# A sparse-attention, mixture-of-experts and feed-forward kernel: local attention of three batches regrouped into units of 18 blocks of 32 queries

## The chip, the cores and the metric

The kernel runs on one core of a Trainium2 chip. The metric is device time in microseconds (us) of one execution, median of several runs.

## The reference

Three stages follow one another on 4 x 576 = 2304 tokens of 512 features, all in f32.

```python
# attention: 4 batches, 8 heads, 576 positions, head size 64
rel = pos[:, None] - pos[None, :]
mask_local = (rel >= 0) & (rel < 32)
mask_strided = (rel >= 0) & (pos[None, :] % 32 == pos[:, None] % 32)
masks = [mask_local for heads 0..3] + [mask_strided for heads 4..7]
attn = softmax(where(masks, q @ k.T / 8, -1e9)); out = attn @ v
# mixture: 8 experts, 1024 wide, weights of the tokens from 8 Sinkhorn rounds over all tokens
out += P[:, e:e+1] * (relu(x @ w1[e]) @ w2[e])
# feed-forward, 2048 wide
h = x @ w_in; return (h * sigmoid(1.702 * h)) @ w_out
```

## The kernel before

The tokens are cut into three blocks of 768. A block passes through the 32 units of the mixture (eight experts, four units of 256 hidden columns each), and later through the units of the feed-forward stage. A unit is a Strassen-like scheme of seven products on two-part (high and low) f32r operands, each product six matmuls of 128x384 (line 1067), and six down products a unit (lines 1333 to 1335). In the code a product or a down product is a *piece*; a unit has 13 places for pieces. `pieces` lists them in order, `advance` runs the next one and the side tasks hung on it (splits of weights, sums of weights on GpSimd, sums of inputs).

The attention of block 0 (batch 0 and the first 192 positions of batch 1) must be there before the first pieces can run on it, and its second half (positions 384 to 767) before the twelfth piece: the first 26 pieces run two units on the first half of the block, then on the second. The rest of the attention is woven between pieces. Heads are taken in pairs; pairs 0 and 1 are local, pairs 2 and 3 strided. A strided ("compact") pair is one group: 64 score products of 32x18 (line 673), mask and maximum on VectorE, one exponential on ScalarE, the sum on VectorE, scaling on GpSimd (line 717), a transpose on VectorE (line 726), copies into `wide`, 16 value products (line 752). A local pair is three groups, each of two tiles of 96 queries against 128 keys, both heads: four score products (line 783), mask and maximum (lines 798, 808), four exponentials with accumulated sums (line 815), scaling on GpSimd (line 830), four transposes on TensorE (line 838), a copy (line 845 or 847), four value products (line 857), a copy into `x` (line 869).

The order is written by hand at the start: `START` is a list of tokens, where S, M, L, E, D, N, T, C, V, K with a group's number are scores, mask, maximum, exponential, sum, scaling, transposes, copy, values and keep; i and a number are that many idle products (line 1480); q and v are loads; W and Y split weights, X the input; P is `advance`. After its 16 pieces `att_step` takes one group a step through a pipeline that is four steps deep, and calls `fill` three times a step, which advances 1.5 pieces on average. After the last step the gate's products and the Sinkhorn rounds follow, between pieces.

TensorE's accumulation banks are few: `pa` serves transposes and one of the two value halves of a compact group, `y` (two buffers) the other half, local values and the down products. Every engine runs its instructions in the written order.

## Time and profile before

| | |
|---|---|
| median of 3 runs | 1942.31 us (1939.58 to 1944.88) |
| the profiled execution | 1940.98 us, span 1939.2 us |
| TensorE (PE) busy | 1907.1 us, 98% |
| VectorE (DVE) | 1454.4 us, 75% |
| GpSimd (POOL) | 1244.9 us, 64% |
| ScalarE (ACT) | 851.8 us, 44% |
| share of the chain that ended last | PE 65%, DVE 2%, POOL 1%, DMA 1% |
| mean granted TensorE clock | 0.997 |

The span is the time from the first to the last instruction of the profiled execution; the shares say how much of it each engine was busy. An engine that is busy all the time bounds the whole, but a share is a mean over stages, so the stages are read apart: rows by windows give each engine's busy time in a stretch, the granted TensorE clock (1.00 is 2.4 GHz, 0.50 is 1.2 GHz) and what the DMA engines moved. An "idle before" with a releaser is a wait, and names who ended it.

### The profile page before, as it was taken

The numbers are of one execution on the slowest core, as the hardware profiler recorded it, in microseconds if no ns is written. First come the engines' busy times: TensorE is split into PE (matmuls) and PEld (weight loads), VectorE is DVE, ScalarE is ACT, GpSimd is POOL, SyncE is SP. The second block draws the span as 40 slices with busy tenths as digits, with TensorE's granted clock in tenths as the row PEclk, the third lists the DMA queues.
The fourth block names the chain that finished last, engine by engine and source line by source line (L and its number), as shares of the span: only waits on it lengthen the run. The fifth ranks groups of instructions, "written<-read, shape, count | busy, mean of one in ns | idle before, by whom it ended". The sixth has DMA issues, their size and how long they took to land.

```text
span 1939.2 us, 35075 instructions
## 1 busy us (share of the span) xinstructions
PE 1907.1 (98%) x11687; PEld 1783.2 (92%) x11687; DVE 1454.4 (75%) x2715; ACT 851.8 (44%) x2079; POOL 1244.9 (64%) x1282
## 2 busy tenths in 40 slices
PE   8999999999999999999999999999999999999999
PEld 6787888888888999999999999999999998888988
DVE  7787687777767788788877788888886766656555
ACT  5555456677664433333333333333333445534332
POOL 4465666777776767677768878888888767601100
PEclk9999999999999999999999999999999999999999
DMA  8477789999997989888888789999989867655653
GB/s 285 146 265 268 257 290 341 353 352 352 353 322 252 333 285 307 291 297 290 288 269 293 255 313 315 319 332 339 347 306 334 284 219 269 239 187 191 223 188 120
DMA packets 284451, 546.18 MB, mean 282 GB/s; under 512 B 30864, under 2 KB 52720, under 8 KB 283376
## 3 DMA queue, kind: packets, MB, share of 16 engines
q1 hardware_dynamic: 280816, 532.08, 79.6%
q10 hardware_dynamic: 3456, 11.87, 1.9%
q8 instruction: 94, 1.54, 0.3%
q14 instruction: 85, 0.70, 0.1%
HBM read 382.30 MB, written 161.53 MB: 280 GB/s over the span
## 4 chain that ended last, share of the span: by engine, by line
PE 65%; DVE 2%; POOL 1%; DMA 1%; issue 0%; ACT 0%; SPq 0%; ACTq 0%; DVEq 0%
PE y L1228 22%; PE pA L1067 18%; PE pC L1067 9%; PE pB L1067 5%; PE y L1335 4%; PE y L1334 4%; PE y L1333 4%; DMA w<-s7moe 1%; DMA w<-s1moe 0%; POOL s L1200 0%; POOL comb L1175 0%; DVE comb L1175 0%; POOL xc L589 0%; DVE xc L593 0%; DVE r L1181 0%
## 5 line engine op out<-in xcount | busy, mean ns | idle before, releaser
L1067 PE MATMUL pA<-xc,w 128*128 128x384 f32 x2880 | 571.9, 335 | 2.7 <-DVE pB L1123 2.1
L1228 PE MATMUL y<-comb,w 128*128 128x384 f32 x2688 | 537.6, 334 | 1.7 <-DVE sum L1238 1.0
L1067 PEld LDWEIGHTS pA<-xc,w 128*128 128x128 f32 x2880 | 507.5, 188 | 20.0 <-DVE pB L1123 3.5
L1228 PEld LDWEIGHTS y<-comb,w 128*128 128x128 f32 x2688 | 472.0, 188 | 3.2 <-DVE sum L1238 2.5
L1175 POOL TENSOR_TENSOR comb<-s,comb 128x384 fp32r<-128x384 f32 x256 | 282.8, 1115 | 88.0 <-ACT comb L1170 79.8
L1238 DVE TENSOR_TENSOR sum<-y,sum 128x384 f32<-128x384 f32 x420 | 230.9, 550 | 96.7 <-PE y L1228 94.6
L1067 PE MATMUL pC<-xc,w 128*128 128x384 f32 x1464 | 295.0, 336 | 0.5 <-issue 0.5
L1335 PE MATMUL y<-w,hl 128*128 128x512 f32 x672 | 268.5, 400 | 4.9 <-DVE hl L1107 4.6
L1067 PEld LDWEIGHTS pC<-xc,w 128*128 128x128 f32 x1464 | 258.9, 188 | 10.5 <-issue 0.9
L1333 PE MATMUL y<-w,hh 128*128 128x512 f32 x672 | 265.0, 394 | 1.6 <-DVE x L869 0.7
L1334 PE MATMUL y<-w,hh 128*128 128x512 f32 x672 | 266.3, 396 | 0.0
L1170 ACT ACTIVATE comb<-r 128x384 fp32r<-128x384 f32 x192 | 101.0, 526 | 364.2 <-DVE r L1181 348.0
L1335 PEld LDWEIGHTS y<-w,hl 128*128 128x128 f32 x672 | 126.5, 188 | 36.2 <-DVE hl L1107 9.0
L1333 PEld LDWEIGHTS y<-w,hh 128*128 128x128 f32 x672 | 126.8, 189 | 21.5 <-DVE acc L1348 1.4
L1067 PE MATMUL pB<-xc,w 128*128 128x384 f32 x708 | 143.2, 337 | 0.0
L1334 PEld LDWEIGHTS y<-w,hh 128*128 128x128 f32 x672 | 126.6, 188 | 15.9
L1175 POOL TENSOR_TENSOR comb<-r,comb 128x384 fp32r<-128x384 f32 x64 | 67.5, 1054 | 114.2 <-ACT comb L1170 114.2
L278 ACT ACTIVATE w<-raw 128x256 fp32r<-128x256 f32 (+1 forms) x307 | 135.7, 460 | 7.2 <-POOL raw L242 6.9
L272 POOL TENSOR_TENSOR w<-raw,w 128x512 fp32r<-128x512 f32 (+1 forms) x104 | 122.3, 1192 | 24.2 <-ACT w L278 23.7
L1170 ACT ACTIVATE comb<-s 128x384 fp32r<-128x384 f32 x256 | 131.6, 514 | 11.0 <-POOL s L1200 11.0
L1200 POOL TENSOR_TENSOR s<-r,r 128x384 f32<-128x384 f32 x127 | 134.3, 1077 | 2.5 <-DVE r L1181 2.0
L1362 DVE TENSOR_TENSOR acc<-y,acc 128x512 f32<-128x512 f32 x126 | 86.7, 688 | 63.1 <-PE y L1335 63.0
(178 smaller groups left out, 2800.4 us busy)
## 6 DMA issues: line engine op xcount, KB each, us to landing
w<-s1moe SPq DMA_DIRECT2D x448, 256.0 KB, 4.9
w<-s7moe SPq DMA_DIRECT2D x448, 256.0 KB, 4.9
s1moe<-w SPq DMA_DIRECT2D x216, 256.0 KB, 5.0
w<-s1ffn SPq DMA_DIRECT2D x133, 256.0 KB, 2.8
s7moe<-kw SPq DMA_DIRECT2D x116, 256.0 KB, 4.7
s7moe<-w SPq DMA_DIRECT2D x96, 256.0 KB, 4.8
w<-s2ffn SPq DMA_DIRECT2D x38, 512.0 KB, 3.8
raw<-wa SPq DMA_DIRECT2D x32, 512.0 KB, 6.0
```

The source lines that it names most:

```text
L272: eng.tensor_tensor(out=t[:, 1], in0=src, in1=f(high), op=ALU.subtract)
L278: nc.scalar.activation(out=high, in_=src, func=AF.Copy)
L1067: nc.tensor.matmul(out=o, lhsT=w[:, hw, kk * P : (kk + 1) * P], rhs=x[:, hx, kk, :], start=opens and m == 0, stop=ends and m == len(todo) - 1,
L1170: nc.scalar.activation(out=t[:, 0, :], in_=part[i, q], func=AF.Copy)
L1175: eng.tensor_tensor(out=t[:, 1, :], in0=part[i, q], in1=f(t[:, 0, :]), op=ALU.subtract)
L1200: eng.tensor_tensor(out=part[i, q], in0=part[i, a], in1=part[i, b], op=op)
L1228: nc.tensor.matmul(out=o, lhsT=t[:, hw, dt * P : (dt + 1) * P], rhs=x[:, hx, :], start=(n == 0), stop=(n == 5))
L1238: nc.vector.tensor_tensor(out=a, in0=o, in1=a, op=ALU.add)
L1333: nc.tensor.matmul(out=o, lhsT=hh[:, c], rhs=w[:, 0], start=(m == 0), stop=False)
L1334: nc.tensor.matmul(out=o, lhsT=hh[:, c], rhs=w[:, 1], start=False, stop=False)
L1335: nc.tensor.matmul(out=o, lhsT=hl[:, c], rhs=w[:, 0], start=False, stop=(m == 1))
L1362: nc.vector.tensor_tensor(out=a, in0=y, in1=a, op=ALU.add)
```

## The change

Batch 0 keeps its local pairs in 96-query tiles (functions now called `tile_...`). In batches 1 to 3 a local pair is one unit: 18 blocks of 32 queries, each against the 64 keys of its own and the previous block, both heads. Scores are 40 products of 32x64 on eight sub-array positions (20 block places, the last two repeated), in the layout [128, 5 x 128]; mask (two instructions) and maximum on VectorE, the subtraction of the maximum on GpSimd, one exponential over 640 columns on ScalarE, the sum on VectorE, the scaling on GpSimd; transposes in two parts (12 blocks in three, 6 blocks in two), written back into `e` by ScalarE; values in 36 products of 64x32 on two sub-array positions. Value tiles of these pairs are laid out anew (18 blocks of 64 keys, 576 KB instead of 384 KB). The compact pairs are as before, with one buffer for their transposed tile instead of two.

The groups become 20 instead of 32, in the order local, compact, local, compact. A step now has four fills of 2.8 pieces and finishes a group one step after its scores. `START` is written anew and goes through 13 groups; it still has 16 pieces, and 34 idle products instead of 24. The tiles' masks are loaded apart, and all masks and constants on SP's queue.

```diff
 START = (
-    "S0 M0 i2 S1 L0 M1 E0 L1 i2 S2 E1 D0 N0 M2 q12 L2 i3 T0:p D1 S4 E2 N1 C0 M4 V0:B L4 T1:p D2 S3 E4 M3 "
...
-    "E9 M10 X3 i2 S12 W211 A2 C7 D9 i1 P1 B1 L10 N9 V7:pB M12 E10 T9 P2 K7 C9 P3 D10 L12 N10 S11 P4 E12 "
-    "M11 L11 P5 Y11 Y10 V9:pB E11 K9 P6 D11 T10:p D12 N11 X6 P7 N12 C10 T11:p S13 V10:B q22 C11 P8 K10 "
-    "M13 V11:B K11 P9 XX21 T12:p S14 P10 L13 C12 P11 E13 M14 P12 S15 q20 D13 i1 P13 L14 N13 M15 E14 L15 "
-    "P14 i3 P15 "
+    "S0 M0 i2 S1 L0 M1 E0 i2 S2 L1 E1 D0 M2 N0 L2 q10 i3 T0:p D1 E2 N1 C0 D2 i2 V0:p S5 K0 N2 T1:p M5 q12 "
...
+    "M9 X3 V6:p E7 S8 D7 v10 q11 L9 q13 K6 P N7 P E9 T7:B M8 "
+    "D9 P P N9 C7 L8 P V7:p Y10 Y11 T9 v11 K7 P S10 C9 M10 P U8 q20 V9:pB E8 S11 L10 D8 P U10 q22 K9 M11 "
+    "P N8 E10 T8:p C8 L11 P V8:p E11 K8 G8:B R8 D11 i1 H8:p D10 N11 S12 v20 T11 q21 N10 M12 C11 J8 i3 "
+    "T10:B L12 G10:p R10 V11:yy U12 C10 V10:p K11 E12 K10 X6 H10:B XX21 v22 J10 i6 P P P P P "
 ).split()
-RATE = 1.5
+RATE = 2.8
...
-        eT = ap.tile([P, 4, P], F32, tag="eT", name="eT")
+        eT = ap.tile([P, 4, P], F32, tag="eT", name="eT", bufs=1)
...
+    def att_scores(i, b, pair):
+        qkt = att_in["qk", b, pair]
+        sc = eps.tile([P, 2, 512], F32, tag="sc", name="sc")
+        for m in range(LM):
+            for c in range(CG):
+                w = min(m * CG + c, NBLK - 1)
+                k0 = max(0, w - 1) * Q
+                for j in range(2):
+                    nc.tensor.matmul(
+                        out=sc[c * Q : (c + 1) * Q, j, m * WIN : (m + 1) * WIN],
+                        lhsT=qkt[j * HD : (j + 1) * HD, 0, w * Q : (w + 1) * Q],
+                        rhs=qkt[j * HD : (j + 1) * HD, 1, k0 : k0 + WIN],
+                        start=True,
+                        stop=True,
+                        tile_position=(j * HD, c * Q),
+                    )
...
+        def below():
+            nc.gpsimd.tensor_tensor(
+                out=s, in0=s, in1=st[:, 0, :, None].to_broadcast([P, 2 * LM, WIN]), op=ALU.add
+            )
...
+    def att_values(i, b, pair, part, banks="y"):
+        av = named_bank(banks[0], "av")
+        lo, hi = (0, PART) if part == 0 else (PART, NBLK)
+        for w in range(lo, hi):
+            for j in range(2):
+                rows = slice(j * HD, (j + 1) * HD)
+                nc.tensor.matmul(
+                    out=av[rows, (w - lo) * Q : (w - lo + 1) * Q],
+                    lhsT=vt[rows, w, :],
+                    rhs=e[rows, w * Q : (w + 1) * Q],
+                    start=True,
+                    stop=True,
+                    tile_position=(j * HD, j * HD),
+                )
...
+    MIXED = (0, 2, 1, 3)
+    groups = [(0, 0, 0), (0, 1, 0), (0, 2), (0, 0, 1), (0, 1, 1), (0, 3), (0, 0, 2), (0, 1, 2)]
+    groups += [(b, pair) for b in range(1, B) for pair in MIXED]
+    NLIST = len(groups) - 4 * (B - 2) + 1
+    NSTEP = len(groups) + 1
...
-        for t in run(2, att_normalise):
-            t()
-        first, apart = run(4, att_values), 4 <= i < n + 4 and groups[i - 4][2] < 0
-        if apart:
-            for t in first:
                 t()
-            first = ()
-            fill()
-        second, third = run(3, att_transpose), run(0, att_scores)
-        for t in first + second:
-            t()
-        if not apart:
-            fill()
-        for t in third[:1]:
-            t()
-        run(1, att_exp)
-        loads_of(i)
+        go(run(1, "normalise"))
+        fill()
+        go(run(1, "transpose", 0))
+        scores = run(0, "scores")
+        go(scores[:1])
+        fill()
+        go(run(1, "transpose", 1))
+        go(run(1, "values", 0))
+        go(scores[1:])
+        fill()
+        go(run(1, "values", 1))
+        run(0, "exp")
         fill()
-        for t in third[1:]:
-            t()
-        fill()
+        loads_of(i)
...
-        nc.scalar.dma_start(out=msk, in_=masks)
+        nc.sync.dma_start(out=spare[1], in_=masks0)
         load_qk(*EARLY[1], begin)
-        nc.scalar.dma_start(out=cst, in_=consts)
...
+        load_qk(0, MIXED[1])
+        nc.sync.dma_start(out=msk, in_=masks)
+        nc.sync.dma_start(out=cst, in_=consts)
```

How the order on the engines moves is seen at three places. First TensorE before the twelfth piece. `pt` are transposes, `av` values, `sc` scores, `idle_out` idle products, `pA` and `pC` products, `y` down products. Before:

```order
L838 MATMUL pt<-cst,e 128x96 x4
L783 MATMUL sc<-qkt 96x128 x4
L1067 MATMUL pC<-xc,w_630 128x384 x6
L1067 MATMUL pA<-xc,w_390 128x384 x6
L1333 MATMUL y<-w_902,hh_938 128x512
```

Now:

```order
L857 MATMUL pt<-cst,e 128x128
L857 MATMUL pt<-cst,e 128x64
L1616 MATMUL idle_out<-idle 128x384
L874 MATMUL av<-e,vt 64x32 x12
L796 MATMUL sc<-qkt 32x64 x40
L1616 MATMUL idle_out<-idle 128x384 x3
L857 MATMUL pt<-cst,e 128x128 x4
L857 MATMUL pt<-cst,e 128x64
L769 MATMUL av<-wide,vc 64x72 x16
L874 MATMUL av<-e,vt 64x32 x36
L1616 MATMUL idle_out<-idle 128x384 x6
L1203 MATMUL pA<-xc,w_367 128x384 x6
```

The eleventh piece (`w_630` before) and the twelfth stood next to each other; now the rest of one unit, the scores of a third, a compact group's values and the whole second half of the second unit stand between pieces, with ten idle products.

Second, GpSimd behind the low part of the first input sum (`xc<-S`). `raw x4` are the sums of one unit's weights, `e<-e,st` the scaling of an attention group, `w` low parts of weights. Before:

```order
L589 TENSOR_TENSOR xc<-S_1064,xc 128x768
L830 TENSOR_TENSOR e<-e,st 96x512
L272 TENSOR_TENSOR w_1106<-raw_790,w_1106 128x256
L242 TENSOR_TENSOR raw_790<-raw_790 128x256 x4
L830 TENSOR_TENSOR e<-e,st 96x512
```

Now:

```order
L594 TENSOR_TENSOR xc<-S_1231,xc 128x768
L277 TENSOR_TENSOR w_1253<-raw_453,w_1253 128x256
L247 TENSOR_TENSOR raw_453<-raw_453 128x256 x4
L843 TENSOR_TENSOR e<-e,st 128x640
L277 TENSOR_TENSOR w_1282<-raw_453,w_1282 128x256
L698 MEMSET e 128x512
```

One scaling is gone from between; the first scaling of the regular steps (batch 2, pair 0) stands behind the sums.

Third, TensorE where it takes up that unit. Before, a regular step:

```order
L1067 MATMUL pC<-xc,w_621 128x384 x6
L857 MATMUL av<-eT,vt 64x96 x4
L838 MATMUL pt<-cst,e 128x96 x4
L783 MATMUL sc<-qkt 96x128 x4
L1067 MATMUL pA<-xc,w_1033 128x384 x6
```

Now, from the eighteenth piece on:

```order
L1203 MATMUL pC<-xc,w_408 128x384 x6
L857 MATMUL pt<-cst,e 128x128 x3
L688 MATMUL sc<-qkt 32x18 x64
L1203 MATMUL pA<-xc,w_499 128x384 x6
```

Before, values, transposes and scores of three different groups stand together; now the transposes of the unit whose scaling was issued one fill earlier, and the scores of the next group.

## Rows read from the trace of the kernel before

**Rows 1.** The page, busy time of the engines over the span.

```profile
PE 1907.1 (98%) x11687; PEld 1783.2 (92%) x11687; DVE 1454.4 (75%) x2715; ACT 851.8 (44%) x2079; POOL 1244.9 (64%) x1282
```

**Rows 2.** Windows: from:to, length, busy PE PEld DVE ACT POOL, clock, DMA, GB/s.

```profile
0.00:69.30 69.30, 57.36 (x962) 45.24 (x962) 51.47 (x118) 40.70 (x138) 31.18 (x37) 1.00 0.67 236
...
69.30:209.30 140.00, 132.44 (x1399) 109.58 (x1398) 103.40 (x228) 73.38 (x235) 84.18 (x103) 0.98 0.70 240
209.30:1939.20 1729.90, 1717.33 (x9328) 1628.43 (x9327) 1299.54 (x2370) 737.73 (x1707) 1129.53 (x1144) 1.00 0.84 287
```

**Rows 3.** TensorE's longest wait in order of time, then the windows around it.

```profile
163.61 0.90 PE L838 MATMUL pt<-cst,e 96*128 96x96 f32 x4 [3.16 <-DVE x L878]
...
162.00:164.00 2.00, 0.39 (x3) 0.40 (x4) 1.60 (x6) 1.27 (x3) 1.84 (x4) 0.79 0.96 361
164.00:166.00 2.00, 2.00 (x133) 1.74 (x131) 0.51 (x1) 1.45 (x7) 1.92 (x4) 0.50 1.04 408
...
168.00:170.00 2.00, 2.00 (x6) 1.58 (x5) 0.91 (x1) 1.31 (x3) 1.38 (x2) 0.50 0.36 133
```

**Rows 4.** The list of waits, TensorE until 330 us: total, times, longest.

```profile
PE pt L838 <- DVE x L878: 5.0, 4, 3.2
```

**Rows 5.** TensorE in order of time (start, us): values, transposes, scores, product.

```profile
78.38 0.55 PE L857 MATMUL av<-eT,vt 128*64 128x96 f32 x8
78.86 0.55 PE L838 MATMUL pt<-cst,e 96*128 96x96 f32 x4
79.34 0.68 PE L783 MATMUL sc<-qkt 64*96 64x128 f32 x8
79.95 1.31 PE L1067 MATMUL pA<-xc,w 128*128 128x384 f32 x6
```

**Rows 6.** The same: compact scores, compact values, gate products, transposes of 128 columns.

```profile
71.17 1.27 PE L673 MATMUL sc<-qkt 64*32 64x18 f32 x128
...
35.80 1.22 PE L752 MATMUL av<-wide,vc 128*64 128x72 f32 x32 [1.59 <-ACT wide L736]
...
81.19 1.51 PE L981 MATMUL pl<-x,wgr 128*32 128x192 f32 x32
...
627.57 0.60 PE L1393 MATMUL px<-cst,acc 128*128 128x128 f32 x4
```

**Rows 7.** Order of time: SP's first issues, VectorE's split, twelfth piece, behind the sixteenth.

```profile
0.74 1.31 SPq L646 DMA_DIRECT2D qkt<-qk  x2
...
60.43 0.95 DVE L589 TENSOR_TENSOR xc<-x,xc 128x768 fp32r<-128x768 f32 x1
...
61.81 1.20 PE L1067 MATMUL pA<-xc,w 128*128 128x384 f32 x6
...
69.34 0.55 PE L857 MATMUL av<-eT,vt 128*64 128x96 f32 x8
```

**Rows 8.** Groups of instructions until 220 us, VectorE and ScalarE: masks, exponentials.

```profile
L798 DVE SCALAR_TENSOR_TENSOR e<-sc,msk 96x512 f32<-96x512 f32 x24 | 16.2, 676 | 6.3 <-PE sc L783 6.0
...
L689 DVE SCALAR_TENSOR_TENSOR e<-sc,msk 128x144 f32<-128x144 f32 x16 | 4.1, 295 | 7.4 <-POOL e L683 5.5 <-POOL e L830 1.2 <-PE sc L673 0.7
...
L815 ACT ACTIVATE e<-e,st 96x128 f32<-96x128 f32 x96 | 37.2, 390 | 10.2 <-DVE st L808 9.3 <-DVE st L827 0.8
```

**Rows 9.** DMA issues until 60 us: size, median us to landing.

```profile
vt<-vw ACTq DMA_DIRECT2D x2, 384.0 KB, 4.4
```

**Rows 10.** GpSimd in order of time: input sum, scaling, weight sums; low parts.

```profile
67.79 1.85 POOL L589 TENSOR_TENSOR xc<-S,xc 128x768 fp32r<-128x768 f32 x1 [2.33 <-DVE e L798]
69.61 1.03 POOL L830 TENSOR_TENSOR e<-e,st 96x512 f32<-96x512 f32 x1
...
71.29 3.15 POOL L242 TENSOR_TENSOR raw<-raw 128x256 f32<-128x256 f32 x4
...
101.04 2.51 POOL L272 TENSOR_TENSOR w<-raw,w 128x512 fp32r<-128x512 f32 x2
```

**Rows 11.** GpSimd in order of time, an idle stretch.

```profile
161.43 0.72 POOL L272 TENSOR_TENSOR dsums<-dsums 128x256 fp32r<-128x256 f32 x1 [6.86 <-ACT dsums L278]
```

More of the change, by code (lines that the diff above doesn't have):

```diff
@@ L638, in strided_attention_moe_ffn @@
     EARLY = ((0, 0), (0, 1))
+    whole = {}
     spare = []
@@ L762, in strided_attention_moe_ffn, with mask, largest @@
     COMPACT = {
-        "att_normalise": compact_normalise,
-        "att_values": compact_values,
-        "att_transpose": compact_transpose,
-        "att_exp": compact_exp,
-        "att_scores": compact_scores,
-    }
+        "normalise": compact_normalise,
+        "values": compact_values,
+        "transpose": compact_transpose,
+        "exp": compact_exp,
+        "scores": compact_scores,
+    }
+    def att_scores(i, b, pair):
[14 more added lines that the diff above has]
+                    )
+        e = ap.tile([P, 2 * LW], F32, tag="e", name="e", bufs=3)
+        st = ap.tile([P, 2, 2 * CQ], F32, tag="st", name="st", bufs=4)
+        s = e.rearrange("p (n k) -> p n k", k=WIN)
+        st = st[:, :, : 2 * LM]
+        att[b, pair] = (e, s, st)
+        def mask():
+            for j in range(2):
+                nc.vector.scalar_tensor_tensor(
+                    out=e.rearrange("p (m c) -> p m c", m=LM)[:, :, j * WIN : (j + 1) * WIN],
+                    in0=sc[:, j, :LW].rearrange("p (m k) -> p m k", k=WIN),
+                    scalar=SCALE,
+                    in1=msk[:, :LW].rearrange("p (m k) -> p m k", k=WIN),
+                    op0=ALU.mult,
+                    op1=ALU.add,
+                )
+        def largest():
+            nc.vector.tensor_reduce(out=st[:, 0, :], in_=s, axis=AX.X, op=ALU.max, negate=True)
+        def below():
+            nc.gpsimd.tensor_tensor(
+                out=s, in0=s, in1=st[:, 0, :, None].to_broadcast([P, 2 * LM, WIN]), op=ALU.add
+            )
+        return mask, largest, below
@@ new lines, in att_exp, with att_normalise, scale @@
+    def att_exp(i, b, pair):
+        e, _, _ = att[b, pair]
+        nc.scalar.activation(out=e, in_=e, func=AF.Exp)
+    def att_normalise(i, b, pair):
+        _, s, st = att[b, pair]
+        den = st[:, 1, :]
+        nc.vector.tensor_reduce(out=den, in_=s, axis=AX.X, op=ALU.add)
+        nc.vector.tensor_scalar_add(den, den, EPS)
+        nc.vector.reciprocal(out=den, in_=den)
+        def scale():
+            nc.gpsimd.tensor_tensor(
+                out=s, in0=s, in1=den[:, :, None].to_broadcast([P, 2 * LM, WIN]), op=ALU.mult
+            )
+        return (scale,)
@@ new lines, in att_transpose, with copy @@
+    def att_transpose(i, b, pair, part, banks="p"):
+        e, _, _ = att[b, pair]
+        pt = named_bank(banks[0], "pt")
+        w, end = (0, PART) if part == 0 else (PART, NBLK)
+        n = 0
+        while w < end:
+            rows = min(CG, end - w) * Q
+            nc.tensor.transpose(pt[:, n : n + rows], e[:rows, w // CG * P : (w // CG + 1) * P], ident[:rows, :rows])
+            w += CG
+            n += rows
+        def copy():
+            nc.scalar.activation(out=e[:, end * Q - n : end * Q], in_=pt[:, :n], func=AF.Copy)
+        return (copy,)
@@ L770, in geometry, with att_keep @@
+    def att_keep(b, pair, q0, n, av):
+        done = 0
+        while done < n:
+            blk, at = divmod(b * S + q0 + done, BT)
+            m = min(n - done, BT - at)
+            nc.vector.tensor_copy(xblk[blk][:, pair, at : at + m], av[:, done : done + m])
+            done += m
     def geometry(g, u):
@@ L795, in att_scores @@
         att[b, pair, g] = (s, st, U, R, C)
+        whole[b, pair, g] = full
         def mask():
@@ L879, in strided_keep @@
             i0 += m
[L882 to L894 removed]
+    LOCAL = {
+        "normalise": att_normalise,
+        "values": att_values,
+        "transpose": att_transpose,
+        "exp": att_exp,
+        "scores": att_scores,
+    }
+    MIXED = (0, 2, 1, 3)
+    TILE = {
+        "normalise": tile_normalise,
+        "values": tile_values,
+        "transpose": tile_transpose,
+        "exp": tile_exp,
+        "scores": tile_scores,
+    }
+    groups = [(0, 0, 0), (0, 1, 0), (0, 2), (0, 0, 1), (0, 1, 1), (0, 3), (0, 0, 2), (0, 1, 2)]
+    groups += [(b, pair) for b in range(1, B) for pair in MIXED]
+    NLIST = len(groups) - 4 * (B - 2) + 1
+    NSTEP = len(groups) + 1
+    pairs = [(b, pair) for b in range(B) for pair in MIXED]
+    at = {p[:2]: i for i, p in enumerate(groups)}
     ring = [p for p in pairs if p[0] > 1 or p[1] < NPAIR // 2]
@@ L1500, in strided_attention_moe_ffn @@
         load_w1(1)
-        for pair in PAIRS[:2]:
+        for pair in MIXED[1::2]:
             load_vc(1, pair)
@@ L1653 @@
         n: np.ascontiguousarray(a)
-        for n, a in dict(qk=qk, vw=vw, vc=vc, wg=wg, wa=wa, wb=wb, wc=wc, wd=wd, masks=masks, consts=consts).items()
+        for n, a in dict(qk=qk, vw=vw, vw0=vw0, vc=vc, wg=wg, wa=wa, wb=wb, wc=wc, wd=wd, masks=masks, masks0=masks0, consts=consts).items()
     }
```

190 lines of the change are left out of this document (111 added, 79 removed), and 6 rows, old and new, of the table START.

## The prediction

> **What bounds the kernel now.** I read the page's first lines, then the busy times of three stretches, then the list of waits, then the order in time of TensorE, VectorE and GpSimd at the places that the change rewrites. TensorE is busy 98% of the span [rows 1], so the time is TensorE's work plus its holes. The holes are early: 11.9 us until 69.3 us (the sixteenth piece's end), 7.6 us from there to 209.3 us (the end of the attention), 12.6 us in the other 1730 us [rows 2]. The change rewrites the first two stretches; the third keeps its instructions, so I take it unchanged, give or take 2 us.
>
> In the second stretch most of the loss is one wait: four transposes wait 3.16 us at 160.45 us for VectorE to clear their bank, and behind it TensorE's granted clock stands at 0.50, that is 1.2 GHz, until 170 us [rows 3]. The row for 162 to 164 us has 0.79, the next three, 2 us each, 0.50: it costs about 0.2 x 2 + 0.5 x 6 = 3.4 us. Holes and clock together are 11.0 us there. In the list of waits, too, VectorE's copies head what TensorE waited for [rows 4].
>
> All sums are made against the profiled execution, 1940.98 us (span 1939.2); the median of the three runs is 1942.31, so I add 1.3 us at the end. A measurement of this kernel can tell about 0.3% (5.8 us) from no change.
>
> **TensorE's work, old tiles.** In the queue's own spacing a group of two 96-query tiles takes 0.61 us of scores, 0.48 of transposes and 0.48 of values [rows 5]: 1.57 us. A pair has three groups, 4.71 us. Six pairs (batches 1 to 3) lose this.
>
> **TensorE's work, new units.** The order shows 40 score products of 64 columns, 5 transposes and 36 value products of 32 columns a pair; an f32 product is issued twice, as the compact scores show (64 products, x128), so 80 and 72 issues.
> - Transposes: four of 128 columns take 0.60 us [rows 6], so 5 x 0.15 = 0.75 us.
> - Scores: the compact scores use the same sub-array positions, 128 issues of 18 columns in 1.27 us, 9.9 ns each [rows 6]. If the sub-arrays overlap, the issue rate binds: 80 x 9.9 ns = 0.8 us. If nothing overlaps, time goes with columns: 64/18 x 9.9 = 35 ns, 2.8 us. The gate's products, also in four column strips, need 47 ns for 192 columns (1.51 us for 32), while the compact values without strips need 38 ns for 72 (1.22 for 32): 0.25 against 0.53 ns a column, so strips do overlap. 64 columns at 0.25 are 16 ns, and the scores use two row halves besides. I take 12.5 ns: 1.0 us.
> - Values: two positions only, weights 64 wide. At best 72 x 9.9 = 0.7 us, at worst the compact values' 38 ns: 2.7 us. I take the middle, some 22 ns: 1.6 us.
>
> A unit is then 3.35 us (bounds 2.25 and 6.25) against 4.71. The Trainium skill speaks against this (TensorEngine Tiling, Instruction Overhead): a matmul carries some 60 cycles whatever its width, so a dimension that is already small should not be tiled. By that, estimated at 25 ns an issue, a unit takes 4.55 us, the stretch behind piece 16 gains 6 us in place of the 9.8 worked out next, and the time is 1936.5, inside the forecast's own range. The 9.9 ns row does not agree with such a floor.
>
> Where this counts: when TensorE has no hole. After piece 16 the kernel before still has 12 score groups, 15 of transposes, 16 of values (22.2 us) and four compact units (1.27 + 1.22 each, 10.0): 32.2 us. The changed one has 3 scores, 4 transposes, 4 values (3.0 + 3.0 + 6.4) and the same 10.0: 22.4 us. **Gain 9.8 us** (bounds: 14 at the cheap ends, nothing at the dear ones).
>
> **The start, up to piece 16.** Before, the twelfth piece starts at 61.81 us, right behind the split of the second half of the input on VectorE [rows 7]. So the start is a chain through VectorE. I priced its queue up to that instruction by row means per element (0.15 us plus 1.04 ns an element, from the 512- and 144-element masks [rows 8]; minute ones 0.2 us): 39.9 us before, 42.1 after, since two whole pairs of batch 1 are now finished where two thirds of one group each were; the idle rest of the 61.4 us is loads and answers from other engines. With the same rest the split ends at 63.5. A walk along the last rungs gives the same: the second unit's mask ends near 45; maximum, subtraction, exponential and sum stand behind other work until 55.4; GpSimd's scaling (1.3 us) ends at 56.8, transposes and copy at 58.7, values at 60.5, copies 60.8, the two high parts (0.83 each) and low parts (0.95) at 63.4. The twelfth piece can start on the first half, at 62.6. It and the next four took 7.5 us before [rows 7], with two score groups (1.2) and four idle products between; I take 6.0 for them alone. So piece 16 ends at about 69 in both: **0 us**, plus or minus 5. The ten added idle products (0.2 us each) lie in this wait and cost nothing unless the wait goes. The second load of masks in front of the second pair's columns on SP costs one issue, 0.65 us [rows 7], at the first rungs; it is inside the plus or minus. The larger value loads (576 KB; one of 384 landed in 4.4 us [rows 9]) are issued a step of some 17 us ahead: nothing.
>
> **The stalls behind piece 16.** A pair's three masks and maxima of 512 elements on VectorE (6 x 0.68 us) become two masks of 320 and two reductions of 640 (2 x 0.48 + 2 x 0.82), and ScalarE's twelve exponentials of 0.39 us one [rows 8]; neither engine bounds, so this only thins the queues. The 3.16 us wait should go: three fills instead of one lie between a compact unit's copies and the next use of that bank. But each unit is now finished one step after it begins, with a single fill (2.8 pieces, 3.4 us) between the sum on VectorE and the transposes, and the scaling between them is on GpSimd, in order. At the first such place the numbers stand in the trace: before, GpSimd's low part of an input sum starts at 67.79 and the four weight sums behind it end at 74.4 [rows 10]; less the old scaling between (1.0), 73.4, which is 4.1 us after piece 16. The new scaling comes right behind these sums and needs 1.3 us; TensorE gets there two pieces, 2.5 us, after piece 16. It waits 4.1 + 1.3 - 2.5 = 2.9 us; counted from the sum that opens the chain, 3.6. I take 3.3 us, as long as the wait that halved the clock before, so I add its 3.4 us. For the other three units I take 1 us each (the weight sums between are partly ready early), for small waits 1.5: 11.2 us in all, against 11.0 us before. **Net 0.**
>
> Sum: 1940.98 - 9.8 + 0 + 0.2 = 1931.4; for the median 1932.7, I say 1932.5. It may be 1923 to 1938 by the single uncertainties.
>
> **Rivals.**
> - *The small products do not overlap.* Two heads' values write one bank, and the compact scores' 9.9 ns could be mere columns (18 at 2.4 GHz are 7.5 ns). For it: no row shows 64-wide sub-arrays. Against: the gate's rows. At 6.25 us a unit the gain is gone and the start grows by some 2: 1944.5, no change. The Trainium skill has this rule (TensorEngine Tiling, Gotcha 1: PSUM Pressure): different row tiles cannot use one bank at once. No run here shows it.
> - *The start's chain ends later.* A dozen rungs on four queues, half a microsecond more on each: the twelfth piece six us later, 1938.5, no change.
> - *GpSimd's scaling becomes the bound, slower.* If at all four units the scaling stands behind a full burst (sums 3.15 us, two low parts 2.5 [rows 10]), each waits 3.5 us and halves the clock: 4 x 6.9 + 1.5 = 29.1 us of stalls against 11.0; 1942.3 - 9.8 + 18.1 = 1950.6. It decides where GpSimd lags by more than the fill less its own 1.3 us, some 2.1 us. Against it: GpSimd stood idle for as long as 6.9 us between such bursts [rows 11].
> - *The stalls go altogether*, and the products cost their low ends: 14 + 8 us, 1920.
>
> That the change does not do what it says is excluded by the order.
>
> **Chances.** Forecast 0.60, no overlap 0.10, later start 0.12, GpSimd 0.12, all stalls gone 0.06. Faster by over 0.3% (below 1936.5): nearly all of the forecast and the last, 0.63; within: 0.23; slower: 0.14. The range 1916 to 1945 leaves out the GpSimd case and tails.
>
> **What would show it.** Score issues near 12 ns and value issues near 22; piece 16's end near 69 us; first transposes behind it waiting near 3 us for GpSimd, with a 0.50 clock behind; end of the attention near 199 us; the rest within 2 us. Wrong, if the second stretch is not shorter by some 10 us, or the start differs by more than 5.

## The result and the profile after

The changed kernel takes 1956.16 us (median of five runs, 1954.26 to 1958.21) against 1942.67 for the kernel before on the same chip: a ratio of 1.0063 with a 95% interval of 1.0050 to 1.0077, slower by about 0.6%. The prediction said 1932.5 us and faster. The profiled execution of after took 1958.21 us, its span is 1956.5.

The page's line of busy times, to be held against [rows 1]:

```profile
PE 1913.8 (98%) x12279; PEld 1796.5 (92%) x12279; DVE 1434.4 (73%) x2666; ACT 828.9 (42%) x1944; POOL 1239.4 (63%) x1276
```

TensorE is 6.7 us busier although it has less to compute, and its idle time grew from 32.1 to 42.7 us. Where that lies is read between landmarks that both programs have: the twelfth piece (the first on the block's second half, [rows 7]) and the gate's products of block 1, which follow the last attention group. Windows of before (from:to, length, busy PE, PEld, DVE, ACT, POOL, clock, DMA share, GB/s); the last row is from the second piece to the twelfth:

```profile
0.00:61.81 61.81, 49.87 (x920) 38.90 (x921) 44.91 (x106) 35.24 (x116) 28.20 (x34) 1.00 0.69 246
61.81:223.27 161.46, 153.78 (x1522) 127.58 (x1521) 119.95 (x258) 84.69 (x270) 98.26 (x118) 0.98 0.68 234
223.27:1939.20 1715.93, 1703.47 (x9248) 1616.76 (x9247) 1289.56 (x2353) 731.87 (x1693) 1118.42 (x1130) 1.00 0.84 287
39.31:61.81 22.50, 19.59 (x177) 15.62 (x177) 16.88 (x37) 12.16 (x39) 9.62 (x9) 1.00 0.48 174
```

The same of after:

```profile
0.00:72.99 72.99, 61.10 (x1261) 50.18 (x1262) 46.29 (x109) 34.74 (x100) 29.80 (x37) 0.88 0.70 245
72.99:243.22 170.23, 152.06 (x1773) 130.83 (x1773) 101.69 (x206) 62.32 (x151) 90.16 (x109) 0.91 0.64 223
243.22:1956.50 1713.28, 1700.62 (x9248) 1615.53 (x9247) 1286.41 (x2353) 731.81 (x1693) 1119.44 (x1130) 1.00 0.84 287
40.78:72.99 32.21, 28.74 (x595) 24.90 (x590) 22.04 (x55) 13.34 (x28) 12.32 (x12) 0.95 0.59 194
```

The start is 11.2 us longer, the stretch of the regular steps 8.8 us longer, where the forecast had it shorter by about 10, and the long rest is 2.7 us shorter. The regular steps have two marks: 18.2 us without TensorE work (7.7 before), and a mean clock of 0.91.

**The steps.** The list of waits for TensorE until 260 us (total, times, longest) has a new head; what stood there before [rows 4] is gone:

```profile
PE pt L857 <- POOL e L843: 14.8, 5, 5.0
PE av L769 <- POOL wide L749: 3.3, 1, 3.3
```

TensorE's first transposes of the four units in order of time (start, us, idle before and who ended it):

```profile
85.82 0.90 PE L857 MATMUL pt<-cst,e 128*128 128x128 f32 x3 [4.33 <-POOL e L843]
...
123.00 0.90 PE L857 MATMUL pt<-cst,e 128*128 128x128 f32 x3 [2.09 <-POOL e L843]
...
160.75 0.90 PE L857 MATMUL pt<-cst,e 128*128 128x128 f32 x3 [2.75 <-POOL e L843]
...
202.37 0.90 PE L857 MATMUL pt<-cst,e 128*128 128x128 f32 x3 [4.96 <-POOL e L843]
```

And GpSimd ahead of the first and the last of them:

```profile
78.13 1.85 POOL L594 TENSOR_TENSOR xc<-S,xc 128x768 fp32r<-128x768 f32 x1 [2.67 <-ACT xc L589]
79.94 0.74 POOL L277 TENSOR_TENSOR w<-raw,w 128x256 fp32r<-128x256 f32 x1
80.64 3.91 POOL L247 TENSOR_TENSOR raw<-raw 128x256 f32<-128x256 f32 x4
84.50 1.26 POOL L843 TENSOR_TENSOR e<-e,st 128x640 f32<-128x640 f32 x1
...
197.01 3.14 POOL L247 TENSOR_TENSOR raw<-raw 128x256 f32<-128x256 f32 x4
200.11 0.98 POOL L277 TENSOR_TENSOR kw<-dsums,kw 128x256 fp32r<-128x256 f32 x1
201.06 1.25 POOL L843 TENSOR_TENSOR e<-e,st 128x640 f32<-128x640 f32 x1
```

The scaling is 1.26 us of work; at the first unit it stands behind 6.5 us of sums and low parts, at the last behind 4.1 ([rows 10] are the same rows of before). How much of a wait is this queue is told by the moment at which the scaling could have begun, the end of the unit's sum on VectorE. Its last step for the four units, with the scaling of the second and third beside it, in order of time:

```profile
80.74 0.22 DVE L840 RECIPROCAL st<-st 128x10 f32<-128x10 f32 x1
...
121.33 0.22 DVE L840 RECIPROCAL st<-st 128x10 f32<-128x10 f32 x1
...
121.69 1.26 POOL L843 TENSOR_TENSOR e<-e,st 128x640 f32<-128x640 f32 x1 [2.08 <-DVE st L840]
...
156.71 0.22 DVE L840 RECIPROCAL st<-st 128x10 f32<-128x10 f32 x1
...
159.26 1.44 POOL L843 TENSOR_TENSOR e<-e,st 128x640 f32<-128x640 f32 x1
...
199.42 0.22 DVE L840 RECIPROCAL st<-st 128x10 f32<-128x10 f32 x1
```

The scaling starts 3.5, 0.1, 2.3 and 1.4 us after it. So GpSimd's queue is about half of the 14.1 us that TensorE waits at the four units. The other half is the scaling itself, and at the second and the fourth unit a sum that ends only after TensorE has stopped (it stops at 120.91 and at 197.41 us): there one fill would be too short with an empty queue too.

The windows of 20 us around the first, third and fourth of these waits show a clock of 0.83, the one around the second 0.91 (not shown), those between them 1.00:

```profile
80.00:100.00 20.00, 15.17 (x251) 12.60 (x251) 7.53 (x16) 3.86 (x9) 8.87 (x11) 0.83 0.30 98
100.00:120.00 20.00, 19.96 (x221) 17.26 (x219) 16.62 (x33) 10.66 (x23) 10.66 (x11) 1.00 0.50 175
...
160.00:180.00 20.00, 19.25 (x264) 16.66 (x265) 9.73 (x20) 7.29 (x20) 9.53 (x14) 0.83 0.83 296
...
200.00:220.00 20.00, 17.63 (x259) 15.26 (x259) 8.69 (x20) 4.04 (x11) 9.49 (x12) 0.83 0.69 240
```

**A unit's work.** TensorE and its weight loads (PEld) in order of time, at full clock:

```profile
39.81 1.04 PE L796 MATMUL sc<-qkt 64*32 64x64 f32 x80
40.78 1.31 PE L1203 MATMUL pA<-xc,w 128*128 128x384 f32 x6
...
60.81 1.59 PE L874 MATMUL av<-e,vt 64*64 64x32 f32 x48
62.33 0.53 PE L857 MATMUL pt<-cst,e 128*128 128x128 f32 x2
```

```profile
60.81 1.48 PEld L874 LDWEIGHTS av<-e,vt 64*64 64x64 f32 x48 [0.26 <-issue]
...
64.09 0.88 PEld L796 LDWEIGHTS sc<-qkt 64*32 64x32 f32 x80
```

From the start of the scores to that of the next product 0.97 us pass, 12 ns an issue, as forecast. 48 value issues take 1.52 us, 32 ns each, and 72 take 2.3 us where 1.6 was forecast. Their weight loads, 64 columns wide, take 31 ns each, those of the scores, 32 wide, 11 ns: values and weight loads keep the same pace.

**The start.** VectorE's masks, sum and copies of the second unit and of what stands ahead of them:

```profile
49.72 0.89 DVE L812 SCALAR_TENSOR_TENSOR e<-sc,msk 128x320 f32<-128x320 f32 x2 [1.16 <-PE sc L796]
...
62.44 0.62 DVE L889 COPY x<-av 128x192 f32<-128x192 f32 x2 [1.38 <-PE av L874]
63.84 0.76 DVE L838 TENSOR_REDUCE st<-e 128x10 f32<-128x640 f32 x1
```

The prediction had this mask end near 45 us and the sum done by 55.4. VectorE idles ahead of both: the mask waits for scores that stand in TensorE's queue until 48.65 us, and the sum stands behind a copy that waits for the first unit's values.

### The profile page after: what moved, and what is told of

Same layout as the page of the kernel before. It is cut to its first block, busy times and chain, and to the rows that moved or that the text cites. A ratio compares the mean times of both kernels' runs of the same rounds, so it can differ in the third digit from the quotient of the medians.

```text
span 1956.5 us, 36063 instructions
## 1 busy us (share of the span) xinstructions
PE 1913.8 (98%) x12279; PEld 1796.5 (92%) x12279; DVE 1434.4 (73%) x2666; ACT 828.9 (42%) x1944; POOL 1239.4 (63%) x1276
## 4 chain that ended last, share of the span: by engine, by line
PE 86%; DVE 5%; POOL 3%; DMA 3%; issue 2%; ACT 1%; SPq 0%; ACTq 0%; POOLq 0%; DVEq 0%
PE pA L1203 23%; PE y L1364 22%; PE pC L1203 12%; PE y L1471 7%; PE y L1470 7%; PE y L1469 7%; PE pB L1203 6%; DMA raw<-wb 1%; DMA s7moe<-kw 1%; PE av L874 1%; DVE w L277 1%; DVE hl L1243 0%; PE av L769 0%; POOL s L1336 0%; DVE xs L578 0%
```

## The experiments

All are edits of the changed kernel; ratios are against the kernel before on the same chip, with 95% intervals. "Gates" is the start of block 1's gate products in the profiled execution (223.27 us before, 243.22 after).

**Unedited, on another chip.**

> The changed kernel itself, unedited, on the same chip as the three beside it, so that they can be compared with it directly. Every theory expects its ratio to the kernel before to be that measured first, 1.005 to 1.008.

Measured: 1954.49 us, 1.0059 [1.0042, 1.0077]; the result stands. Its profiled execution has the twelfth piece at 74.58 and the gates at 239.70 us. In the six profiled executions with the same written order the twelfth piece starts at 69.2 to 74.6 us, so single executions don't tell 2 us apart there.

**The weight splits later.**

```diff
-    "L5 C1 W210 T2 E5 i5 V1:p W220 D5 S4 W110 Y01 M4 W120 C2 K1 i2 S3 ...
+    "L5 C1 T2 E5 i5 V1:p W210 W220 D5 S4 W110 Y01 M4 W120 C2 K1 i2 S3 ...
```

> Only the written list of the start is edited: the first weight split (W210) comes behind the exponential of the second compact group and the values of the second tile group, instead of in front of them on ScalarE. If ScalarE was held by that split, whose data landed at 21.2 us (8.94 us of waiting in the changed kernel), the exponential of the compact group runs near 17.5 us instead of 21.5, the 3.15 us wait of the fourth score group (24.0 us) goes, the clock does not fall to 0.50 at 24 us, piece 16 ends near 74 us instead of 78.9, and the time falls by 4 to 7 us, to about 1950. If the start is instead held by the arrival of the loads themselves, piece 16 still ends within 1.5 us of 78.9 and the time stays at 1956.

Measured: 1957.14 us, 1.0070 [1.0048, 1.0092]. The twelfth piece stands at 69.92 us, the gates at 238.01, but the time didn't move, where 4 to 7 us had been expected if this was the cause. ScalarE was held by a split whose weights had not landed (8.94 us idle in after), and is still held 2.88 us ahead of the splits. It is not the cause of the lost time, or too little of it to see.

**The units' scaling on VectorE, and the transposes one fill later.** The first takes GpSimd's queue out of the way, the second keeps it and gives it time:

```diff
-            nc.gpsimd.tensor_tensor(
+            (nc.vector if i >= NLIST - 1 else nc.gpsimd).tensor_tensor(
                 out=s, in0=s, in1=den[:, :, None]..., op=ALU.mult)
```

> The scaling of the four units of the regular steps moves from GpSimd to VectorE; nothing else changes. If TensorE's transposes wait because the scaling stands behind weight sums in GpSimd's queue, the four long waits (4.3, 2.1, 2.8 and 5.0 us) fall below 0.7 us each, the granted clock stays at 1.00 from 80 to 240 us, and the time falls by 20 to 28 us, to 1929 to 1936. If instead one fill between sum and transposes is too short whatever the engine (the chain through VectorE), the waits stay over 2 us each and the time is above 1948.

```diff
         fill()
-        go(run(1, "transpose", 0))
         scores = run(0, "scores")
         go(scores[:1])
         fill()
-        go(run(1, "transpose", 1))
-        go(run(1, "values", 0))
+        go(run(1, "transpose", 0))
         go(scores[1:])
         fill()
-        go(run(1, "values", 1))
+        go(run(1, "transpose", 1))
+        go(run(1, "values", 0))
         run(0, "exp")
         fill()
+        go(run(1, "values", 1))
```

> In the regular steps the first transposes come one fill later (behind the mask and the second fill), the other parts of the unit move along, and the last values come behind the fourth fill; engines and instructions are the same. If the distance of one fill is what is too short for GpSimd's queue, the waits on the scaling fall below 1 us each and the time falls by 18 to 26 us, to 1930 to 1938. If the queue were simply too full (GpSimd the bound), the wait would only move and the time would stay above 1950.

Measured: 1949.44 us, 1.0027 [1.0012, 1.0042] for the first; 1944.66 us, 0.9999 [0.9985, 1.0013] for the second. Neither gives what was expected of it (20 to 28 us and 18 to 26 us). On VectorE the wait is halved but not gone (list of waits, until 260 us):

```profile
PE pt L857 <- DVE e L843: 6.7, 4, 3.7
```

What is left is long at the second and fourth unit, 1.64 and 3.68 us, where the sum itself was late; at the first and third it is 0.60 and 0.74.

With the transposes later no wait for the scaling is left in the steps, and the windows between the landmarks read (the last row is from the second piece to the twelfth):

```profile
0.00:69.16 69.16, 59.36 (x1260) 48.59 (x1261) 44.61 (x109) 34.58 (x100) 31.13 (x37) 0.90 0.73 259
69.16:221.30 152.14, 142.83 (x1773) 122.32 (x1772) 105.79 (x206) 62.01 (x151) 90.56 (x109) 0.99 0.69 240
221.30:1938.80 1717.50, 1703.03 (x9248) 1616.65 (x9247) 1288.17 (x2353) 732.64 (x1693) 1120.17 (x1130) 1.00 0.83 287
39.91:69.16 29.25, 27.62 (x593) 23.59 (x589) 22.16 (x55) 13.13 (x28) 12.85 (x13) 1.00 0.66 225
```

The second row is the gain that was forecast: 152.1 us where before had 161.5, with 9.3 us of idle time and the clock at 0.99. Moving a unit's transposes, and its values with them, by one fill of 2.8 pieces took off 0.6 points of ratio, the whole loss as far as these intervals tell. The start is still 7.4 us longer than before, which uses the gain up.

**Idle products in the waits.** Is it the wait or the halved clock behind it?

```diff
+        if part == 0 and i >= NLIST - 1:
+            for _ in range(10):
+                nc.tensor.matmul(out=pt[:, : 2 * P], lhsT=ident, rhs=cst, start=True, stop=True)
```

> Ten idle products of 128x256 into the transposes' own bank stand in front of the first transposes of each of the four units; the scaling and its place stay. This takes the pause away but not the lateness. If the halved clock behind each wait is a cost of its own, the clock stays at 1.00 from 80 to 240 us and the time falls by 8 to 14 us although the transposes start no earlier; if the clock matters little, the time stays within 3 us of 1956.

Measured: 1957.19 us, 1.0057 [1.0042, 1.0072], no gain, though the clock stayed up, at 1.00 in each window of 20 us from 80 to 220 us; one of them:

```profile
160.00:180.00 20.00, 20.00 (x281) 17.47 (x280) 10.88 (x22) 7.67 (x20) 10.79 (x15) 1.00 0.92 324
```

The gates stand at 239.33 us, 3.9 earlier than in after and 0.4 earlier than in its other execution; 8 to 14 us had been expected if the halved clock is a cost of its own. But the run doesn't settle that. A group of idle products lasts 4.48 us, longer than the second and the third wait, and there the products themselves hold the transposes back: at the second unit the scaling ended at 122.40 us, the transposes start 2.1 us later (at the third unit 1.3 us):

```profile
120.21 4.48 PE L856 MATMUL pt<-cst 128*128 128x256 f32 x20
124.52 0.49 PE L860 MATMUL pt<-cst,e 128*128 128x128 f32 x3
```

What a halved clock costs is seen at the last compact group, behind which no scaling is due. After the same wait TensorE runs the same instructions without a pause up to the gates' products. In after (mean clock 0.79 from the first start to the second):

```profile
229.90 2.19 PE L769 MATMUL av<-wide,vt 128*64 128x72 f32 x32 [3.32 <-POOL wide L749]
...
243.22 1.51 PE L1117 MATMUL pl<-x,wgr 128*32 128x192 f32 x32
```

In its other execution, on another chip (mean clock 1.00):

```profile
228.96 1.22 PE L769 MATMUL av<-wide,vt 128*64 128x72 f32 x32 [3.29 <-POOL wide L749]
...
239.70 1.51 PE L1117 MATMUL pl<-x,wgr 128*32 128x192 f32 x32
```

That is 13.32 against 10.74 us: one fall of the clock costs 2.6 us there. In the steps a part of such a loss lies in time in which TensorE would wait for the next scaling anyway; how much is not shown.

**Both moves together, then the compact copies all on ScalarE.** The transposes are later as above, and the splits go further back; the second run also takes GpSimd's share of the copies into `wide` away:

```diff
-    "L5 C1 W210 T2 E5 i5 V1:p W220 D5 S4 W110 Y01 M4 W120 C2 K1 i2 S3 L4 M3 E4 i2 ...
+    "L5 C1 T2 E5 i5 V1:p D5 S4 M4 C2 K1 i2 S3 L4 M3 W210 W220 W110 E4 Y01 W120 i2 ...
```

```diff
-                if c % 2 and i >= NLIST:
+                if False:
```

> Both edits together: the weight splits of the start behind the exponential of the second compact group and the masks of the next groups (further back than in the first try, where ScalarE was then held in front of a compact group's copies), and the transposes of the regular steps one fill later. If the two losses are apart (a held ScalarE in the start, the scaling's place in GpSimd's queue in the steps), they add: piece 16 ends near 74 us, the last gate products near 215 us, and the time is 6 to 8 us below the one with the later transposes alone, ratio to before 0.996 to 0.998. If the start is bound by its loads or by the two whole units that stand in front of the twelfth piece, piece 16 ends within 2 us of the 78.9 of the changed kernel and the ratio stays near 1.000.

> As the run before, and the compact groups' four copies in the regular steps all on ScalarE instead of half on GpSimd. If what is left of waits on GpSimd's queue costs time, the waits of the compact values on these copies (3.6 us in three) go and the time falls by another 2 to 4 us; if they are covered, it stays within 1 us of the run before.

Measured: 1943.03 us, 0.9996 [0.9982, 1.0010], and 1942.74 us, 0.9998 [0.9982, 1.0013]. The splits add nothing to be seen, where another 6 to 8 us had been expected if the two losses were apart. In the second the wait for `wide` only changes its releaser (3.7 us in four waits for ScalarE).

**Values: bank or weight load?** First the two heads' values in two banks (with a copy of its own out of each), then each product cut into two of 32 columns of weights:

```diff
-                    out=av[rows, (w - lo) * Q : (w - lo + 1) * Q],
+                    out=avs[j][rows, (w - lo) * Q : (w - lo + 1) * Q],
```

> In the regular steps the two heads' values of a unit go to two banks instead of one; the start is as it was. In the changed kernel 48 value issues took 1.52 us from start to start, 32 ns each, where I had taken 22. If the shared bank keeps the two sub-array positions apart, the steps' issues fall to 16 to 20 ns (48 in about 0.9 us); if the weights (64 columns a product) or the missing overlap of the two positions set the pace, they stay near 32 ns.

```diff
+            for d in range(0, HD, Q):
-                    out=av[rows, (w - lo) * Q : (w - lo + 1) * Q],
-                    lhsT=vt[rows, w, :],
+                    out=av[j * HD + d : j * HD + d + Q, (w - lo) * Q : (w - lo + 1) * Q],
+                    lhsT=vt[rows, w, d : d + Q],
-                    tile_position=(j * HD, j * HD),
+                    tile_position=(j * HD, j * HD + d),
```

> The changed kernel, each value product of a unit cut into two of 32 columns of weights (144 issues instead of 72 a unit). Theory 'the issue rate of values is that of their weight loads' (in the changed kernel 48 value issues take 1.52 us and their loads of 64x64 weights 1.48 us, 31 ns each; the scores' loads of 64x32 take 0.88 us for 80, 11 ns each): 96 issues of the first part take about 1.1 to 1.2 us instead of 1.52, a unit 1.6 to 1.75 us instead of 2.3. Rival 'an issue of values costs 32 ns whatever its weights': 96 issues take 3 us. The time moves by less than can be told in one look, since the units wait for their scaling anyway.

Measured, the first (1963.49 us, one execution), TensorE in order of time:

```profile
92.11 1.59 PE L875 MATMUL av<-e,vt 64*64 64x32 f32 x48
```

The second (1954.84 us, one execution), TensorE, then weight loads:

```profile
58.12 1.02 PE L875 MATMUL av<-e,vt 64*32 64x32 f32 x96
```

```profile
58.12 0.91 PEld L875 LDWEIGHTS av<-e,vt 64*32 64x32 f32 x96 [0.25 <-issue]
```

Two banks change nothing: 48 issues still take 1.59 us. With strips twice as many issues take a third less, 1.02 us, 10.6 ns each, and the loads fall from 31 to 9.5 ns. That the weight load was the price is the best reading, but the cut changes two things at once: the width of a load, and the number of sub-array positions, four instead of two. For the width speak the scores, whose loads are as wide as the strips' and which run on eight positions: they take 12 ns, so twice the positions gain nothing. (TensorEngine Tiling (Array Packing), Gotcha 1: PSUM Pressure, in the Trainium skill, says that different row tiles can't use one bank at once; this run doesn't show such a cost here. The Trainium skill's page TensorE: Matmul & The Clock Gate, LDWEIGHTS, says that a load's time goes with its columns, columns/1.2 ns: the rows agree that columns count, 31 against 11 ns, not with the 53 ns that this gives for 64.)

**The start written anew**, from the second unit's maximum on; then also SP's first loads in another order, and strips everywhere:

```diff
-    ... C9 M10 P U8 q20 V9:pB E8 S11 L10 D8 P U10 q22 K9 M11 "
+    ... C9 M10 L10 P U8 q20 V9:pB E8 U10 S11 D8 P E10 N8 q22 K9 M11 "
-    "P N8 E10 T8:p C8 L11 P V8:p E11 K8 G8:B R8 D11 i1 H8:p D10 N11 S12 v20 T11 q21 N10 M12 C11 J8 i3 "
-    "T10:B L12 G10:p R10 V11:yy U12 C10 V10:p K11 E12 K10 X6 H10:B XX21 v22 J10 i6 P P P P P "
+    "P T8:p C8 D10 N10 L11 P V8:p E11 K8 G8:B R8 D11 i1 H8:p N11 T10:B C10 T11 S12 v20 q21 J8 G10:p R10 C11 "
+    "V10:B i1 K10 M12 V11:yy L12 U12 K11 X6 XX21 E12 v22 H10:p J10 i5 P P P P P "
```

```diff
-        load_qk(*EARLY[0], rest)
-        load_qk(*EARLY[1], rest)
         load_v(*EARLY[0])
         load_qk(0, MIXED[3])
-        load_vc(0, MIXED[1])
         load_v(*EARLY[1])
+        load_qk(*EARLY[1], rest)
+        load_vc(0, MIXED[1])
+        load_qk(*EARLY[0], rest)
```

> The version with the weight splits and the transposes later, and with its start from the second unit's maximum on written anew: maximum, sum and scaling of the second unit directly one after another, its first values ahead of the last compact group's, its second values (not needed by block 0) behind. Theory 'the twelfth piece is late by the way through the second unit, rung by rung, since VectorE, GpSimd and TensorE do other groups' work between its rungs': the twelfth piece starts near 67.3 us instead of 69.8, and the time falls by 2 to 3 us from 1943.0, to some 1940.5. Rival 'TensorE's own work sets it from 40 us on (it is busy 31 of 32 us between 40 and 72)': the twelfth piece stays within 1 us of 69.8 less the 0.8 us of the moved values, and the time within 1 us of 1942.5.

> The same with two edits more: the order of SP's loads (first values and the fourth pair's columns ahead of the second halves of the first two pairs' columns), and the value products in strips of 32 columns of weights. Theory 'loads in the wrong order hold the first rungs': the waits of 1.6 us for the first values and 2.75 us for the fourth pair's columns go or fall under 1 us, the clock stands higher between 16 and 40 us, and the first piece starts 2 to 3 us earlier than 37.7 us. With the strips (0.6 us less work a unit, six units, 3.6 us) the time is near 1935. Rival 'the early waits are hidden before the twelfth piece': the twelfth piece is no earlier than in the run with the new tail but for 1.2 us of cheaper values, and the time 1937 to 1938. If the strips cost 32 ns each instead, values grow by 2.3 us a unit and the time goes to some 1950.

Measured: 1942.68 us, 0.9992 [0.9978, 1.0005], with the twelfth piece at 72.12 us, later instead of earlier; and 1944.63 us, 1.0002 [0.9987, 1.0017], with it at 73.72. The last groups' ways are interlocked: in the first the last compact group's values now end behind the units' values that block 0 needs. The loads in another order moved a wait, since the third tile's scaling came later (TensorE, in order of time, the second kernel):

```profile
30.06 0.90 PE L963 MATMUL pt<-cst,e 96*128 96x96 f32 x4 [6.29 <-POOL e L955]
```

**Strips in the steps alone**, on the version with both moves: the one version whose interval lies below that of the kernel before.

```diff
+        n = Q if i >= NLIST - 1 else HD
-            for d in range(0, HD, Q):
+            for d in range(0, HD, n):
```

> The version with the weight splits and the transposes later, and the values of the four units in the regular steps in strips of 32 columns of weights (144 issues a unit at 10 to 12 ns, in place of 72 at 32 ns); the written order keeps the undivided form, since there a wait for issue of 1.64 us stood behind two strip groups. Theory 'with the scaling out of the way TensorE's own work sets the steps': four units save 0.6 to 0.7 us each, so the gates of block 1 start 2.5 us earlier than 220.16 us and the time falls from 1943.0 to some 1940.5, ratio 0.998. Rival 'the steps are set by copies and by waits for issue': the gates stay within 1 us of 220, the ratio stays at 0.9995 to 1.0.

Measured: 1940.15 us over 11 runs, 0.9983 [0.9973, 0.9992], faster than before by 0.17%. It is the best of eight versions that have the later transposes, whose ratios run from 0.9983 to 1.0003, so a part of this may be luck of the choice. That the strips do it is not shown: against the version without them (0.9996) the intervals overlap, and in the profile the gates stand at 223.22 us, not earlier. From the twelfth piece on the stretch is as long as without strips, 150.6 against 150.3 us, though TensorE is busy 1.3 us less in it.

**What holds the start.** On that version: first, what the twelfth piece does not need (second transposes and values of both units, the next unit's scores) goes behind it; second, without the ten idle products of the last groups.

```diff
+    "P N8 E10 T8:p C8 L11 P V8:p D10 N10 E11 K8 D11 N11 T10:B C10 T11 C11 i1 V10:p K10 V11:yy K11 X6 XX21 i6 "
+    "P G8:B R8 H8:p J8 P S12 M12 L12 U12 v20 q21 P G10:B R10 H10:p J10 E12 P v22 P "
```

> The version with strips in the steps, with its written order changed at the end: the second unit's sum and scaling directly behind its exponential, and what block 0 does not need (both units' second values with their transposes, the next unit's scores with mask, maximum and exponential) behind the twelfth piece, between the last four. Theory 'the late twelfth piece is TensorE's own queue, that is work moved ahead, and no loss': the stretch from the second piece to the twelfth falls from 29.3 us to about 26 to 27, TensorE's work in it by 2.7 us (scores 1.0, values 0.8, second transposes 0.9), and the time stays within 2 us of 1940.2. Rival 'a late twelfth piece is lost time': the time falls by as much as the stretch, to some 1937.5. Third: the way through the last compact group (copies on ScalarE, then 16 products) holds the stretch at 29 us whatever TensorE has to do, and TensorE stands idle for 2 to 3 us more in it: time 1942 to 1943.

> The version with strips in the steps, without the ten idle products between the second unit's values and the twelfth piece. Theory 'they lie in waits': the twelfth piece stays where it is relative to the second piece (29.3 us), TensorE's idle time before it grows by some 2 us, and the time stays within 1 us of 1940.2, unless the clock falls behind the holes (then up to 3 us more). Rival 'they are in the way': the stretch shortens by up to 2.2 us and the time with it, to some 1938.

Measured: 1943.67 us, 1.0003 [0.9990, 1.0016], and 1942.49 us, 0.9992 [0.9978, 1.0006]. In the first the stretch from the second piece to the twelfth stays at 29.5 us (windows):

```profile
40.33:69.86 29.53, 27.00 (x460) 23.55 (x454) 20.23 (x50) 11.94 (x25) 11.01 (x11) 0.84 0.46 160
```

Without that work the stretch is no shorter than the 29.3 us of the version without strips, though shorter than the 32.6 us in the profiled execution of the version that it edits; one execution each can't tell these apart. In it the second unit's transposes wait 1.38 us for the scaling, the last compact group's values come only behind its own scaling, transpose and copies and end at 67.8 us, and the mean clock is 0.84. That fits the third theory best, and nearly its time (1942 to 1943), but TensorE's idle time is 2.5 us against 1.7 in the version without strips, not 2 to 3 us more. In the second the stretch is 28.1 us (41.18 to 69.30; one matmul of the twelfth piece runs already at 68.34, the other five wait for the input until 69.30). The idle products lay partly in waits and partly in the way; the time fits neither theory well.

## Why the prediction was wrong, point by point

- **Stalls behind piece 16, "Net 0".** The mechanism was right and the first size nearly: the first wait was given as 3.3 us behind the input sum and the four weight sums, and is 4.33. The step that failed is "For the other three units I take 1 us each (the weight sums between are partly ready early)": they are 2.09, 2.75 and 4.96, and idle time in this stretch grew from 7.7 to 18.2 us. GpSimd's queue holds the scaling for 3.5, 2.3 and 1.4 us at the first, third and fourth unit; at the second GpSimd had been idle for 2.08 us, and there and at the fourth VectorE's sum came after TensorE had stopped. So the rival that GpSimd's scaling becomes the bound came in part, and its argument against (GpSimd idle 6.9 us between bursts, [rows 11]) spoke of a place where nothing was due; the late sums stand in no rival. What the runs show as cause is the distance of one fill: with the transposes one fill later the ratio is 0.9999 in place of 1.0063. GpSimd's queue alone is not all of it: with the scaling on VectorE it is 1.0027.
- **The clock, "3.4 us" a wait.** The size was about right: one fall costs 2.6 us where nothing hides it. But the sum adds it once, for the first wait; it fell behind all four (0.83, 0.91, 0.83, 0.83 over 20 us) and behind the last compact group's. What these falls cost in the steps, where the next scaling may set the pace anyway, stays open.
- **The start, "0 us, plus or minus 5".** It is 7 to 13 us over the six executions. The failed step is the walk along the last rungs, which began with "the second unit's mask ends near 45": it ends at 50.6, since the scores stand in TensorE's queue until 48.65. I priced VectorE's queue and took its idle rest as the same; the rungs also pass TensorE's order and ScalarE's copies, and between the second piece and the twelfth TensorE has 8 us more to do at full clock (27.6 us in the run with the later transposes, whose start is written as in after, against 19.6 before). That was half in the prediction's own numbers: six units at its own price save 8.2 us in all, and 9.8 were booked behind piece 16, so 1.6 had to come in ahead of it, and 2 of idle products. The experiments leave it there: moving the late weights, the loads or the unneeded work, or leaving out idle products, did not give the start back, and what holds it stays open.
- **Values, "some 22 ns: 1.6 us".** 32 ns, 2.3 us: the middle between two bounds, without the row that decides, the weight loads. A unit costs 4.0 to 4.2 us (0.97, 0.7 to 0.9 for the transposes, 2.3), so a pair saves 0.5 to 0.7 us, not 1.36. By the prediction's sum behind piece 16 that is some 7 in place of 9.8 us.
- **Scores, "1.0 us"** (0.97) held, **and the rest unchanged** nearly (1713.3 against 1715.9 us, 2.7 where 2 were allowed; 1717.5 with the transposes later). A small misreading that moves nothing: in the 7.5 us from the twelfth piece to the sixteenth's end before stands one score group, not two. For the rule of TensorEngine Tiling, Instruction Overhead, in the Trainium skill, the prediction estimated 25 ns an issue from its 60 cycles: 12 ns an issue, and 10.6 in the strips, are under half of that. Counted by the f32 product, which is two issues, they are 24 and 21 ns, near that estimate, so which of the two the rule means decides whether the rows agree.
- **The sum** then reads 11.2 us later at the twelfth piece, 8.8 more to the gates, 2.7 less behind: 17.3 between the two profiled spans, 13.5 between the medians.

## What to carry to other kernels

When a producer moves closer to its consumer, ask at every place what stands ahead of it on the producer's queue, and when its own input is ready; take the worst place, not the queue's mean idle time. Here one fill more of distance, with the same instructions on the same engines, gave back the whole loss, and a faster place for the producer only half of it. When work is written earlier in an order, charge it there and credit it once. Price many small products by their weight loads too: a weight tile of 32 columns in place of 64 made twice as many products a third cheaper.

## What was not expected of the hardware

- Cutting a 64x32 value product in two makes it cheaper: 31 ns for a load of 64x64 weights, 9.5 to 11 ns for one of 64x32.
- Behind nearly the same wait (3.32 and 3.29 us) of the same program the clock fell in one execution and not in the other, and the same instructions took 13.32 and 10.74 us. Holding the clock up with idle products gained nothing, but these also stood in the way.
- In both executions of the changed kernel TensorE waits 1.89 us inside a run of small products with no releaser in the profile ("issue"); in the four others whose start is written the same way such a wait is 0.85 us or less. It may be part of the scatter of the start. In after:

```profile
54.54 1.29 PE L688 MATMUL sc<-qkt 64*32 64x18 f32 x110 [1.89 <-issue]
```

What ends that wait stays open.
